# A new order of operations on every engine for a fused attention and MLP kernel

## The chip, the cores and the metric

The kernel runs on one core of a Trainium2 chip. The metric is the device time of one execution in microseconds; the time before is the median of three runs.

## The reference, cut to what matters

The input x is 2048 rows (S) of 448 columns (D) in bfloat16. Two blocks follow each other.

```python
h  = x + A(layernorm(x))          # local attention, 16 heads of 28, 8 keys at distances 0, 2, ..., 14
h2 = h + B(layernorm(h))

A: q, k, v = split(x @ wqkv)
   logits[s, w] = q[s] . k[s - 2w] / sqrt(28);  attn = softmax over w
   return (sum_w attn[s, w] * v[s - 2w]) @ wo

B: g = gelu(layernorm(x) @ w1);  shift the four quarters of g's columns by +1, -1, +2, -2 rows
   x1 = x + shifted(g) @ w2
   return x1 + gelu(layernorm(x1) @ w3) @ w4      # 448 -> 1792 -> 448
```

## The kernel before

The 2048 rows are worked in four tiles of 512 (t = 0 to 3), the last part of the MLP in five units of 256, 512, 512, 512 and 256 rows (u = 0 to 4). The phases of one tile carry names that the text uses:

- **N1, A1, V** (per t): layernorm of x; its transposition; q and k; v. The evicted v goes to `vt`, and up to four DMAs copy it with shifts into `vw`.
- **A2, S, A3, O**: A2 multiplies q by the shifted k on DVE (four products into `qk_r`; the three large ones 128 x 4096) and sums over the head on PE. S is the softmax; its last step is a product into `pb` that may run on DVE or on POOL. A3 spreads the weights on DVE (four products into `bd_r`) and multiplies them by `vw` on PE. O is the projection by wo and the residual.
- **B1, M**: two layernorms in one, normalisation into `lntm`, a transposition by DMA into `actT`, then the matmuls by w1 with gelu.
- **B2, T, W3, B3** (per u): shifted matmuls by w2 and the residual; layernorm and a transposition by DMA; the matmuls by w3 with gelu into `h3T`; the matmuls by w4, the last addition into `ost` and the DMA to the output.

All operations are first recorded, 891 of them, numbered 0 to 890 in the order of the phases. One number is an instruction or a group of matmuls. Then a list written out in the source, `ORDER` (line 19), gives the sequence: each engine works its own operations in that sequence, one after the other, and an operation that waits holds up all behind it on its engine. `OTHER` (line 51) names the operations that go to their second engine: an eviction from ACT to DVE, or a product from DVE to POOL. The list also decides which buffer an operation gets, since buffers are handed out and taken back along it: 8 PSUM banks, 3 `bd_r`, 2 `qk_r`, 2 `lntm`, 4 `actT`, 16 `h3T`.

All DMAs are issued by SP, in the order of the list. A transposition by DMA is kept apart from the loads and copies around it: `arrange` (lines 192 to 240) makes it wait until all of those ahead of it have landed, and makes those behind it wait until it has landed. Stores to the output are exempt.

```python
            if op.insts[0][0] == "dma_start_transpose":
                op.deps.update(turned + moved)
                turned, moved = [op], []
            elif op.is_dma and not callable(op.chan):
                op.deps.update(turned)
                moved.append(op)
```

All instructions are issued at line 994, so the profile's groups are told apart by the names of their tiles. The numbers that the text uses:

| number | what | engine before |
|---|---|---|
| 98, 101, 104, 106 | evictions of the first transposition (A1, t = 0) | ACT; 104 DVE |
| 127, 129 | evictions of the last q and k columns (t = 0) | DVE; ACT |
| 160, 161; 279, 280; 401, 402 | last step of the softmax's sum on ACT, and the product into `pb`, of S0, S1, S2 | 161 and 280 DVE, 402 POOL |
| 253 | copy of 128 x 48 in the arena (t = 1) | ACT |
| 256, 378, 379, 383 | evictions of v (t = 1, 2) | ACT |
| 368 | eviction of 64 x 256 (A1, t = 2) | ACT |
| 457 to 461 | variance of x for t = 3 (four squares, a logarithm) | ACT |
| 388, 390 | the first two large products of A2, t = 2 | DVE |
| 404, 521; 534, 411 | evictions of S2 and S3; of A3, t = 3 and 2 | ACT; 411 DVE |
| 505, 509 | large products of A2, t = 3; 506 and 510 are the matmuls on them | DVE |
| 420, 421, 424, 425 | residual of O, t = 2 | DVE |
| 200, 322, 440, 557 | transpositions of B1, t = 0 to 3, issued to M0, M1, M2, M3 | SP |
| 586, 649, 720, 791, 850 | transpositions of T, u = 0 to 4, issued to W3 | SP |
| 582, 583; 641 to 644 | normalisation of T0; of T1 | DVE |
| 501, 502, 503, 504 | copies of v of t = 3 into `vw` (16, 256, 320 and 48 KB) | SP |
| 35, 36; 37, 38 | loads of w3 (896 KB each); of w4 (784 KB each) | SP |
| 527, 528 | one of the A3 matmul groups of t = 3 and its eviction | PE; DVE |
| 617 | third of the four matmul groups of B3, u = 0 | PE |

Of the kernel before, what the change touches and what calls it, by code (L numbers as in the profile page):

```python
# [16 lines left out]
POWER = {'N1': 'aaaa', 'B1': 'aaaa', 'B2': 'apapp'}  # L17
RESIDUAL = 'ttvv'
ORDER = """
# [30 lines left out]
"""  # L50
OTHER = """
104 127 196 197 199 402 408 411 519 525 528 582 583
"""
FULL = (4,)
FILL = (1, 1, 0, 0)
# [980 lines left out]
```

## Time and profile before

| | |
|---|---|
| runs before | 194.11 us median (193.75 to 195.71, three runs) |
| span of the profiled execution | 192.0 us, 5741 instructions |
| PE, DVE, ACT, POOL busy | 181.2, 129.6, 133.0, 29.3 us |
| DMA moved | 17.04 MB, 89 GB/s in the mean |

The span runs from the first to the last instruction of the program; of the profiled execution the page gives the span alone, and the runs are longer than it by what lies before and after. A matmul's busy time overlaps with that of the next, so PE's share alone says little; whether one group follows the other without a hole is read from the rows in order of time. Groups of the view by line give a count, the busy time, the mean of one in ns and the idle time ahead of it.

### The profile page before, as it was taken

How to read it: one execution, taken by the hardware profiler on the slowest of the kernel's cores; microseconds unless marked ns; L12 is line 12 of the kernel's file. 1: busy time of each engine (PE TensorE's matmuls, PEld its weight loads, DVE VectorE, ACT ScalarE, POOL GpSimd, SP SyncE). 2: the span in 40 equal slices, each digit the busy share in tenths (PEclk: the TensorE clock that was granted, in tenths of full speed). 3: DMA queues.
4: the chain of work that ended last, by engine and by line, in shares of the span. 5: the costliest groups of instructions: out<-in, count | busy, mean ns of one | idle time of the engine just before them, and what ended most of it. 6: DMA issues, size and time to landing. Idle time of an engine off the chain costs nothing.

```text
span 192.0 us, 5741 instructions
## 1 busy us (share of the span) xinstructions
PE 181.2 (94%) x2482; PEld 92.6 (48%) x2482; DVE 129.6 (67%) x229; ACT 133.0 (69%) x310; POOL 29.3 (15%) x63
## 2 busy tenths in 40 slices
PE   6999999999999869969999999999999999999994
PEld 2584533453444333337545444455444544555672
DVE  7899999999999999999876970036988022002203
ACT  4489999999999999998595898860158004731340
POOL 3240000000004000201067000022077700000000
DMA  5998792005504163935905014006200542000111
GB/s 146 353 282 175 194 295 44 14 0 133 133 3 90 23 66 72 319 64 125 113 3 106 8 34 103 0 0 126 58 26 1 109 106 73 0 3 0 51 48 48
DMA packets 30273, 17.04 MB, mean 89 GB/s; under 512 B 18936, under 2 KB 29736, under 8 KB 30248
## 3 DMA queue, kind: packets, MB, share of 16 engines
q1 hardware_dynamic: 30248, 16.68, 37.1%
q8 instruction: 19, 0.31, 0.7%
q14 instruction: 6, 0.05, 0.1%
HBM read 8.04 MB, written 1.84 MB: 51 GB/s over the span
## 4 chain that ended last, share of the span: by engine, by line
PE 67%; DMA 13%; ACT 12%; DVE 3%; SPq 2%; issue 1%; POOL 0%; POOLq 0%; ACTq 0%
PE ps L994 67%; DMA actT<-lntm 7%; DMA arena<-in_B_w_dram 3%; ACT lntm L994 3%; ACT arena L994 3%; DMA vw<-vt 2%; ACT vt L994 2%; SPq L994 2%; DVE bd_r L994 2%; ACT h3T L994 1%; ACT actT L994 1%; ACT xin L994 1%; DVE lntm L994 1%; DVE ost L994 1%; ACT ls L994 1%
## 5 line engine op out<-in xcount | busy, mean ns | idle before, releaser
L994 PE MATMUL ps<-actT,arena 64*128 64x256 bf16 (+1 forms) x756 | 68.7, 329 | 2.2 <-DMA actT<-lntm 1.7
L994 ACT ACTIVATE h3T<-ps 128x512 bf16<-128x512 f32 (+1 forms) x70 | 30.3, 525 | 40.1 <-PE ps L994 40.0
L994 PEld LDWEIGHTS ps<-actT,arena 64*128 64x128 bf16 x756 | 35.4, 94 | 31.6 <-DMA actT<-lntm 2.1
L994 PE MATMUL ps<-arena,h3T 64*128 64x448 bf16 (+2 forms) x434 | 44.4, 343 | 0.0
L994 ACT ACTIVATE arena<-ps 128x512 bf16<-128x512 f32 (+10 forms) x86 | 40.1, 515 | 3.3 <-PE ps L994 2.5
L994 DVE SCALAR_TENSOR_TENSOR ost<-ps,mrs,arena 128x448 bf16<-128x448 f32 (+1 forms) x17 | 10.7, 652 | 36.5 <-PE ps L994 36.5
L994 DVE TENSOR_TENSOR qk_r<-arena 128x4096 bf16<-128x4096 bf16 (+1 forms) x16 | 32.0, 2016 | 0.4 <-ACT arena L994 0.2
L994 PEld LDWEIGHTS ps<-arena,h3T 64*128 64x128 bf16 (+1 forms) x434 | 23.0, 94 | 18.7 <-issue 0.2
L994 POOL TENSOR_TENSOR arena<-arena,xin 128x448 f32<-128x448 f32 x16 | 17.2, 1088 | 45.0 <-DVE lntm L994 45.0
L994 DVE TENSOR_TENSOR bd_r<-arena,bmask 80x2048 bf16<-80x2048 bf16 x16 | 19.0, 1216 | 1.6 <-PE ps L994 0.9
L994 ACT ACTIVATE actT<-ps 128x512 bf16<-128x512 f32 (+2 forms) x21 | 14.6, 742 | 2.1 <-PE ps L994 2.1
L994 PE MATMUL ps<-actT,w_s 64*128 64x512 bf16 x112 | 13.3, 377 | 1.7 <-DMA actT<-lntm 1.2
L994 PE MATMUL ps<-wo_s,actT 64*128 64x448 bf16 x128 | 14.3, 350 | 0.1
L994 PE MATMUL ps<-arena,actT 64*128 64x448 bf16 x112 | 12.4, 350 | 0.4 <-ACT vt L994 0.4
L994 PE MATMUL ps<-w_s,arena 64*128 64x448 bf16 x112 | 11.6, 350 | 1.0 <-ACT arena L994 0.9
L994 ACT ACTIVATE lntm<-xin,nm 128x448 bf16<-128x448 bf16 x16 | 10.5, 660 | 2.6 <-DVE nm L994 2.6
L994 DVE SCALAR_TENSOR_TENSOR arena<-xin,rs_y,ps 128x448 f32<-128x448 bf16 x16 | 10.3, 672 | 2.2 <-PE ps L994 2.2
L994 DVE TENSOR_SCALAR lntm<-arena,mv,rs_y 128x512 bf16<-128x512 f32 x14 | 10.2, 773 | 2.1 <-POOL rs_y L994 2.0
L994 POOL TENSOR_TENSOR pb<-ls,mx 128x512 bf16<-128x512 f32 x2 | 3.3, 1641 | 52.8 <-ACT mx L994 52.8
L994 DVE BATCH_NORM_STATS2 st<-xin 128x6 f32<-128x448 bf16 x16 | 9.4, 614 | 0.8 <-DMA xin<-in_A_x_dram 0.7
L994 PEld LDWEIGHTS ps<-actT,w_s 64*128 64x128 bf16 x112 | 5.1, 94 | 8.9 <-PE ps L994 1.7
L994 PEld LDWEIGHTS ps<-wo_s,actT 64*128 64x128 bf16 x128 | 5.6, 94 | 6.7 <-PE ps L994 1.4
(73 smaller groups left out, 161.7 us busy)
## 6 DMA issues: line engine op xcount, KB each, us to landing
arena<-in_B_w_dram SPq DMA_DIRECT2D x2, 896.0 KB, 7.3
out_dram<-ost SPq DMA_DIRECT2D x15, 112.0 KB, 1.9
arena<-in_B_w_dram SPq DMA_DIRECT2D x2, 784.0 KB, 5.7
vw<-vt SPq DMA_DIRECT2D x4, 320.0 KB, 4.3
vw<-vt SPq DMA_DIRECT2D x4, 256.0 KB, 4.2
arena<-in_A_wqkv_dram SPq DMA_DIRECT2D x2, 448.0 KB, 4.6
xin<-in_A_x_dram SPq DMA_DIRECT2D x2, 448.0 KB, 7.5
xin<-in_A_x_dram SPq DMA_DIRECT2D x3, 224.0 KB, 5.6
```

Source lines behind the costliest of these rows:

```text
L994: inst = getattr(eng, meth)(**kw)
```

## The change

Only `ORDER` and `OTHER` are replaced. No operation, buffer count or constant changes. Two lines of the old list and two of the new, and `OTHER` in full:

```diff
 ORDER = """
-43 8 7 2 11 0 1 49 44 45 6 9 10 12 5 39 13 40 42 58 59 60 61 63 64 62 70 68 50 51 52 53 54 55 56 57 14 65 66 71 69 67
-72 73 75 77 97 15 98 99 100 102 105 74 76 103 101 41 113 119 104 106 46 212 125 218 126 84 107 214 114 216 129 130 215
 ...
+0 1 49 50 51 52 53 54 55 56 57 39 40 2 7 5 42 8 58 59 60 61 11 9 63 64 62 65 66 10 68 70 71 67 69 6 41 72 73 74 75 97
+82 99 4 92 100 102 103 105 12 13 77 76 96 106 98 101 107 119 104 14 212 214 15 218 216 120 125 121 126 127 130 133 219
 ...
 OTHER = """
-104 127 196 197 199 402 408 411 519 525 528 582 583
+106 129 161 196 197 199 253 280 368 383 402 404 408 519 521 525 528 534 582 583
```

From `OTHER`: 106, 129, 253, 368, 383, 404, 521 and 534 go from ACT to DVE; 104, 127 and 411 go back to ACT; 161 and 280 go from DVE to POOL.

From `ORDER`, engine by engine, the places that the text speaks of:

```text
SP   before: ... 30..34 | 143 35 145 36 262 144 | 265 | 387 264 263 384 385 386 | 200 | 322 | 504 37 501 38 | 586 | 503 502 | 440 | 649 ...
SP   after:  ... 144 262 143 145 20 21 22 264 23 265 263 24..32 386 33 34 35 387 384 36 385 | 200 | 504 | 322 | 503 | 586 | 501 37 38 502 | 440 | 649 ...
DVE  before: ... 158 272 161 270 463..466 ... 277 388 392 280 390 185 ...
DVE  after:  ... 158 272 270 253 383 464 463 466 465 ... 277 388 368 390 392 185 ...
DVE  before: ... 505 308 310 304 306 (305 307 309 311) 412 406 415 321 320 319 318 409 509 574 575 576 411 507 408 581 425 424 511 583 582 420 421 ...
DVE  after:  ... 505 308 310 306 304 (311 309 307 305) 404 415 319 321 318 320 409 412 511 406 574 575 576 507 408 581 424 582 583 509 421 425 420 ...
PE   before: ... 615 616 | 530 533 524 | 447 441 448 442 (M2) | 527 | 617 | 535 539 536 540 | 618 | B22, W31 ...
PE   after:  ... 615 616 | 524 533 | 617 | 447 441 448 442 (M2) | 530 527 | 618 | 539 535 540 536 | B22, W31 ...
```

The bars on SP stand where a transposition and other DMAs wait for each other. In the tail (from W31 on) the matmul groups of W3, B3 and B2 change places among themselves, with their evictions.

56 rows, old and new, of the table ORDER are left out of this document.

## The prediction

> **What bounds the kernel now.** I read the page's shares first, then the busy time in five stretches, then the chain that ended last, then the single queues.
>
> ```profile
> span 192.0 us, 5741 instructions
> 13.80:63.60 49.80, 48.33 (x857) 22.51 (x854) 49.43 (x61) 49.42 (x130) 2.21 (x1) 1.00 0.46 109
> 63.60:85.70 22.10, 17.88 (x278) 7.04 (x278) 21.17 (x40) 21.69 (x47) 1.32 (x2) 1.00 0.52 114
> 85.70:96.10 10.40, 9.89 (x240) 7.08 (x242) 9.04 (x16) 7.54 (x23) 1.24 (x2) 1.00 0.68 110
> 96.10:192.00 95.90, 93.35 (x988) 48.46 (x988) 38.83 (x85) 46.56 (x93) 19.26 (x21) 1.00 0.20 45
> ```
>
> The columns are length, then PE, PEld, DVE, ACT and POOL busy. Up to 63.6 us DVE and ACT are full (49.4 of 49.8), and so nearly up to 85.7; PE has room there. From 96.1 on PE alone is full and nothing else is near it. So there are two kernels here: a front paced by the order on DVE and ACT, and a tail that is 96 us of matmuls without a hole, which a new order can't shorten, only start earlier or break. The chain tells what sets its start:
>
> ```profile
> 58.34 0.70 ACT lntm L994
> 64.01 3.49 DVE bd_r L994 x3
> 67.50 1.29 DVE lntm L994 x4
> 68.82 5.27 DMA actT<-lntm
> 74.78 0.57 SPq L994
> 76.09 6.49 DMA arena<-in_B_w_dram
> 82.60 3.06 DMA actT<-lntm
> 85.71 2.49 PE ps L994 x42
> 90.60 5.43 DMA actT<-lntm
> 96.07 92.72 PE ps L994 x981
> ```
>
> These are the transposition of B11 (68.82), the two loads of w4 (37 and 38, issued at 74.78 and 76.09), the transposition of T0 that had to wait for them (82.60), W30 (85.71), the transposition of B12 (90.60) and M2 (96.07), where the dense tail begins.
>
> **The change, part by part.** The work is the same 891 operations. I follow the new order up to M2 and ask how late or early each of those points comes.
>
> Engines. Two softmax products (161, 280) go from DVE to POOL, eight evictions or copies go from ACT to DVE, and three come back.
>
> ```profile
> L994 DVE TENSOR_TENSOR pb<-ls,mx 128x512 bf16<-128x512 f32 x2 | 1.4, 682 | 0.0
> L994 DVE CAST actT<-ps 128x512 bf16<-128x512 f32 x4 | 2.7, 683 | 0.0
> L994 DVE CAST arena<-ps 64x256 bf16<-64x256 f32 x1 | 0.4, 383 | 0.0
> 31.36 1.22 DVE L994 TENSOR_TENSOR qk_r<-arena 128x2048 bf16<-128x2048 bf16 x1
> 32.49 0.68 DVE L994 TENSOR_TENSOR pb<-ls,mx 128x512 bf16<-128x512 f32 x1
> 33.09 2.29 DVE L994 TENSOR_TENSOR qk_r<-arena 128x4096 bf16<-128x4096 bf16 x1
> ```
>
> Back to back, a DVE operation takes 0.08 less than its length (32.49 to 33.09 is 0.60 for one of 0.68). The pairs 104/106 and 127/129 only change places. Ahead of the normalisation of B10 DVE loses 161 and 280 (2 x 0.60) and gains 383 (0.55, from the 683 ns row scaled to 448), 368 (0.30) and 253, a copy of 128x48 that no row has on DVE (0.1 to 0.3, I take 0.2): -0.15 in sum. That is next to nothing on an engine that is full. ACT is relieved by the same three, which matters at B10 alone (below).
>
> The products on POOL are not free for DVE, though.
>
> ```profile
> 42.86 4.48 DVE L994 TENSOR_TENSOR qk_r<-arena 128x4096 bf16<-128x4096 bf16 x2
> 58.98 2.28 DVE L994 TENSOR_TENSOR qk_r<-arena 128x4096 bf16<-128x4096 bf16 x1
> 59.99 2.21 POOL L994 TENSOR_TENSOR pb<-ls,mx 128x512 bf16<-128x512 f32 x1 [47.99 <-ACT mx L994]
> 86.13 1.07 POOL L994 TENSOR_TENSOR pb<-ls,mx 128x512 bf16<-128x512 f32 x1 [4.84 <-ACT mx L994]
> 98.47 1.86 DVE L994 TENSOR_SCALAR lntm<-arena,mv,rs_y 128x512 bf16<-128x512 f32 x2 [1.14 <-POOL rs_y L994]
> 98.55 1.04 POOL L994 TENSOR_TENSOR arena<-arena,xin 128x448 f32<-128x448 f32 x1
> ```
>
> The product takes 1.07 when DVE reads PSUM beside it (86.13) and 2.21 when a DVE product of two SBUF tensors is under way (59.99: that one ends at 61.26, and 61.26 + 1.0 is where POOL ends). At 98.47 it is DVE that waits: two operations take 1.86 beside a POOL addition. So 280, whose input comes while 388 runs, waits for it and then holds up 390, since an eviction (368) stands between them and lets POOL in: 0.7 of its 1.07 on DVE. 161 comes some 2.5 later than the 32.49 of before (an estimate), because ACT now does 378, 256, 379, 460 and 461 ahead of 160; it meets 270's end and blocks the normalisations for 0.3. With the -0.15 and waits of 0.1 in the first 40 us, that is 0.95, and I say that DVE is 0.9 late by 505, which then ends at 62.1 instead of 61.26. If POOL takes nothing from DVE it is level; if each of 161, 280 and 402 takes its whole 1.07, it is 3.1 late. I take 0.9, the value nearest to the row at 59.99.
>
> [...]
>
> B10. Its transposition (200) waited at 58.34 + 0.70 = 59.04 for ACT's share of the normalisation, while DVE's was done at 58.3. Now ACT's is early and DVE's ends at 58.3 + 0.9 = 59.2. M0 comes at 63.6, as before. Ahead of 200 the SP queue now has the load of w3 behind V2's copies, which wait for A30 (43 by my walk); 2.5 MB at the pace of w4 below end at 56, 3 us to spare, and without them each microsecond costs one.
>
> B11 and T0. From 505's end to 322's issue it was 68.82 - 61.26 = 7.56. Two of the three bd products (3.49) now stand behind the normalisation and 404 (0.60) ahead of it: 5.83. So 322 is issued at 67.9 instead of 68.82 and lands at 73.2. T0's normalisation:
>
> ```profile
> 69.85 2.28 DVE L994 TENSOR_TENSOR qk_r<-arena 128x4096 bf16<-128x4096 bf16 x1
> 76.91 0.62 DVE L994 SCALAR_TENSOR_TENSOR xin<-ps,xin 128x448 bf16<-128x448 f32 x1
> 79.35 1.00 DVE L994 TENSOR_SCALAR lntm<-arena,nm,rs_y 128x512 bf16<-128x512 f32 x2
> 80.98 3.06 PE L994 MATMUL ps<-w_s,arena 64*128 64x448 bf16 x28 [0.23 <-ACT arena L994]
> 85.68 1.38 SPq L994 DMA_DIRECT2D vw<-vt  x2
> ```
>
> It ended at 80.35. Ahead of it are no longer 509 (2.20), 411 (0.60) and 425 (0.54), but 404 (0.60) and the 0.9: 78.5, less 0.4 for DVE's holes in that stretch, 78.1. 509 now comes behind it and ends at 80.3; the matmuls on it (510) come ahead of B21 on PE. So B21 starts at 81.0, as before (80.98), and W30 is free to start 2.65 later (B22, of the same size, goes from 105.35 to 108.00 below), at 83.65.
>
> The loads. 586 is issued at 78.1, with 503 landed before it (73.2 + 4.2), and lands 3.06 later, at 81.2. That is ahead of 83.65, so W30 starts at 83.65 instead of 85.71: **2.05 won**. But w4, 501 and 502 are now behind 586, and B12's transposition (440) waits for all of them. Before, w4 went from 74.78 to 82.58: 7.8. Now: 81.2, one short copy, w4 from 81.9 to 89.7, and 502 behind it.
>
> ```profile
> vw<-vt SPq DMA_DIRECT2D x4, 256.0 KB, 4.2
> DMA to landing us min/median/max: 2.2/4.2/8.3
> DMA to landing us min/median/max: 3.0/4.4/5.4
> ```
>
> The second row is that of vw, the third that of actT. 502 has 256 KB. At w4's pace (1568 KB in 7.8) it adds 1.3, and 440 is issued at 91.0; it takes 8.3 at the most from its issue at 83.2, 91.5; it adds its whole 4.2 if it runs only when w4 is done, 93.9. I take 91.0. B12's normalisation itself is ready a little earlier, at 90.3 by the same count of DVE's operations. 440 took 5.43 in this place, so M2 starts at 96.4 instead of 96.07. Of the 2.05 nothing is left there.
>
> What stays is work done ahead of M2.
>
> ```profile
> 96.07 3.20 PE L994 MATMUL ps<-actT,w_s 64*128 64x512 bf16 x28 [0.43 <-DMA actT<-lntm]
> 99.20 0.42 PE L994 MATMUL ps<-bd_r,vw 80*32 80x64 bf16 x32
> 99.55 1.50 PE L994 MATMUL ps<-arena,h3T 64*128 64x448 bf16 x14
> 105.35 2.81 PE L994 MATMUL ps<-w_s,arena 64*128 64x448 bf16 x28
> 108.00 10.74 PE L994 MATMUL ps<-actT,arena 64*128 64x512 bf16 x98
> ```
>
> 617 (1.44, from 99.55 to 100.99) now goes ahead of M2, one more A33 group (0.3) behind it. From M2 to B22 it was 9.28; it becomes 8.14, so B22 starts at 104.5 instead of 105.35. W31, 2.65 later, needs T1's transposition: DVE's 528 stands ahead of three of T1's four normalisations and waits for 527 on PE (about 100), so 649 is issued at 102.2 to 103.1 and lands 4.4 later, at 106.6 to 107.5. W31 starts at 107.25 instead of 108.00. This wait is a cover that is nearly gone: each later microsecond of 649 costs one.
>
> The tail. From W31 on the same matmuls follow. Walking banks, transpositions and gelus, I find the next tight place at W32, about 1 us of slack for T2 (its last normalisation now stands behind an operation on B23). I cost it at nothing; without the slack it costs what T2 is late.
>
> The sum: 192.0 - 0.75 = 191.25 in the span. The median of the runs is 194.11, 2.1 more than the span; that lies around it and stays: 191.25 + 2.1 = **193.4 us**. An error of 1 us in 440's issue moves it by 1.
>
> **The rivals.**
>
> 1. *Faster, 191.9.* POOL takes nothing from DVE (T0 at 77.2) and 440 takes the median 4.4 instead of 5.43. Then not the landing but PE starts M2, at about 95.0, 1.4 earlier than in the sum. For it: B11's and B12's are the only long ones of nine. Against: B12's stood behind copies then as it will now.
>
> 2. *Slower, 196.3.* The copy 502 makes no headway until w4 is through: 89.7 + 4.2 = 93.9, M2 at 99.3, B22 at 107.4, W31 at 110.1 or a little later, 2.2 behind: 192.0 + 2.2 + 2.1. For it: copies of vw have taken up to 8.3, and w4 alone takes 7.8. Against: two of them together took only 4.9 (issued at 85.68, and 440, which waited for both, at 90.60). It costs time from M2 later than 97.1 on, and over 1% from 99.0.
>
> 3. *Little, but slower, 195.5.* POOL gets its turn after every DVE product, and 161, 280 and 402 cost DVE 3.1 instead of 0.9. T0, and with it w4 and M2, come 2.2 later: 193.4 + 2.2 - 0.1. The rows at 42.86 and 33.09 show how close the DVE products stand, for it; against it, 160 is so late that 161 meets fewer of them.
>
> 4. *The change doesn't do what it says, 194.1.* DVE is full and its work is the same; the w4 move wins at W30 what it loses at M2, and 649 takes the rest.
>
> **How the numbers follow.** The forecast with its own range of 192.6 to 194.3 gets 0.36, rival 4 0.10, the first 0.18, the second 0.24, the third 0.12. A change under about 1% (1.9 us) can't be told from none here: faster is the first rival and a little of the forecast (0.20), slower the second and a quarter of the third (0.27), the rest is within it (0.53). Range 191.3 to 196.6: from below rival 1 to above rival 2.
>
> **What would show it.** Right: W30 at about 83.6, with T0's transposition issued before w4; DVE rows beside POOL's pb lengthened; 440 at 91, waiting for a DMA; PE full from M2 on, with at most a short wait at W31. Wrong: B10's transposition waiting for w3, B21 later than 82, a hole at W32, or B12's normalisation later than 91.

## The result and the profile after

The changed kernel takes 203.76 us (median of four runs, 203.37 to 204.92) beside 194.06 for the kernel before in the same series: ratio 1.0488, 95% interval 1.0430 to 1.0545. It is slower by 9.7 us, where 193.4 (191.3 to 196.6) was predicted. Its profiled execution has a span of 201.5 against 192.0. First the page of the changed kernel: the busy time, and the granted clock in 40 slices.

```profile
PE 185.8 (92%) x2482; PEld 95.2 (47%) x2482; DVE 130.7 (65%) x232; ACT 134.4 (67%) x305; POOL 38.5 (19%) x65
PEclk9999999999979997899999999999999999999999
```

DVE and ACT have about as much work as before (130.7 and 134.4 against 129.6 and 133.0); PE has 4.6 us more busy time for the same 2482 matmuls, and the clock row is lowered in three slices, at two places. The busy time in stretches of the changed kernel, cut at the same events as before (start of the dense front, M0, W30, M2, end); the last three columns are the granted clock, the DMA share and GB/s:

```profile
13.80:71.10 57.30, 51.35 (x855) 22.98 (x856) 49.91 (x59) 51.56 (x130) 8.88 (x4) 0.97 0.39 101
71.10:93.40 22.30, 18.68 (x280) 7.64 (x282) 20.46 (x39) 20.44 (x40) 1.27 (x1) 0.92 0.32 68
93.40:105.40 12.00, 11.32 (x224) 7.39 (x222) 11.85 (x25) 11.04 (x28) 3.90 (x3) 1.00 0.65 178
105.40:201.50 96.10, 92.70 (x1008) 49.84 (x1004) 37.72 (x83) 44.06 (x90) 19.17 (x21) 1.00 0.23 45
```

The lengths were 49.8, 22.1, 10.4 and 95.9: the loss is 7.5 ahead of M0, 0.2 up to W30, 1.6 up to M2, and 0.2 in the tail. In the first stretch DVE does as much as before (49.9 against 49.4) in 7.5 us more, so it stands idle there; the clock is 0.97 and 0.92 where it was 1.00. The chain that ended last in the changed kernel shows which waits are new:

```profile
47.00 6.29 POOL pb L994
...
79.67 7.31 PE ps L994 x84
87.01 2.87 DVE qk_r L994
...
111.34 5.61 DMA actT<-lntm
```

A POOL product, PE itself in the middle of the front, and a product of DVE stand where the chain of before, from 43.07 to 85.71, had ACT, short stretches of DVE, copies, the loads of w4 and the transpositions. The pieces around 47 in the changed kernel, by engine in order of time. A row gives start, length, engine and operation, and in brackets how long the engine had stood idle and what ended it:

```profile
35.82 1.48 POOL L994 TENSOR_TENSOR pb<-ls,mx 128x512 bf16<-128x512 f32 x1 [23.69 <-ACT mx L994]
36.29 1.05 DVE L994 COPY arena<-arena 128x48 bf16<-128x48 bf16 x1
...
45.34 2.27 DVE L994 TENSOR_TENSOR qk_r<-arena 128x4096 bf16<-128x4096 bf16 x1
47.00 6.28 POOL L994 TENSOR_TENSOR pb<-ls,mx 128x512 bf16<-128x512 f32 x1 [9.70 <-ACT mx L994]
47.54 0.41 DVE L994 CAST arena<-ps 64x256 bf16<-64x256 f32 x1
47.87 4.47 DVE L994 TENSOR_TENSOR qk_r<-arena 128x4096 bf16<-128x4096 bf16 x2
53.43 0.49 PE L994 MATMUL ps<-ident,pb 64*80 64x64 bf16 x16 [2.92 <-POOL pb L994]
54.88 1.76 PE L994 MATMUL ps<-arena,actT 64*128 64x448 bf16 x8
56.38 0.17 DVE L994 TENSOR_SCALAR nm<-mv 128x4 f32<-128x4 f32 x1 [4.04 <-ACT xin L994]
```

Operation 280 has its input at 47.00 and ends at 53.28. It got its turn neither at the end of 388 (47.61) nor beside the eviction 368 (47.54) nor between 390 and 392; it ends 0.94 after the end of the last of them (52.34). Transposition 281 on PE needs it and stood first on that queue for 2.92; the matmuls of O0 stand behind 281, their results go through ACT, and DVE's next operation, 185, waited 4.04 for those. 161 (35.82) takes 1.48 on POOL, and the copy 253 beside it 1.05.

### The profile page after: what moved, and what is told of

It reads as the page before. It is cut to its first block, busy times and chain, and to the rows that moved or that the text cites. A ratio compares the mean times of both kernels' runs of the same rounds, so it can differ in the third digit from the quotient of the medians.

```text
span 201.5 us, 5745 instructions
## 1 busy us (share of the span) xinstructions
PE 185.8 (92%) x2482; PEld 95.2 (47%) x2482; DVE 130.7 (65%) x232; ACT 134.4 (67%) x305; POOL 38.5 (19%) x65
## 4 chain that ended last, share of the span: by engine, by line
PE 53%; ACT 19%; DVE 18%; DMA 4%; POOL 3%; issue 2%
PE ps L994 53%; ACT arena L994 10%; DVE qk_r L994 4%; ACT actT L994 3%; POOL pb L994 3%; DMA actT<-lntm 3%; DVE lntm L994 3%; DVE bd_r L994 2%; DVE st L994 2%; DVE arena L994 2%; ACT lntm L994 2%; DVE mx L994 1%; ACT vt L994 1%; ACT xin L994 1%; DMA xin<-in_A_x_dram 1%
## 5 line engine op out<-in xcount | busy, mean ns | idle before, releaser
L994 PE MATMUL ps<-actT,arena 64*128 64x512 bf16 (+1 forms) x756 | 69.6, 329 | 1.6 <-DMA actT<-lntm 0.8
L994 PEld LDWEIGHTS ps<-actT,arena 64*128 64x128 bf16 x756 | 36.2, 94 | 30.7 <-PE ps L994 2.0
L994 ACT ACTIVATE arena<-ps 128x512 bf16<-128x512 f32 (+9 forms) x83 | 39.6, 507 | 10.7 <-PE ps L994 9.7
L994 PE MATMUL ps<-arena,h3T 64*128 64x448 bf16 (+2 forms) x434 | 45.5, 343 | 0.0
L994 POOL TENSOR_TENSOR arena<-arena,xin 128x448 f32<-128x448 f32 x16 | 18.3, 1154 | 58.0 <-DVE lntm L994 58.0
L994 POOL TENSOR_TENSOR pb<-ls,mx 128x512 bf16<-128x512 f32 x4 | 9.9, 2477 | 56.4 <-ACT mx L994 56.4
L994 DVE TENSOR_SCALAR lntm<-arena,mv,rs_y 128x512 bf16<-128x512 f32 x14 | 8.0, 610 | 12.7 <-ACT rs_y L994 12.1
L994 PE MATMUL ps<-arena,actT 64*128 64x448 bf16 x112 | 13.8, 369 | 0.4 <-ACT arena L994 0.2
L994 PE MATMUL ps<-w_s,arena 64*128 64x448 bf16 x112 | 13.3, 373 | 0.4 <-ACT arena L994 0.3
L994 DVE SCALAR_TENSOR_TENSOR arena<-xin,rs_y,ps 128x448 f32<-128x448 bf16 x16 | 10.4, 676 | 3.8 <-PE ps L994 3.7
L994 PE MATMUL ps<-qk_r,zc 128*32 128x512 bf16 x112 | 8.7, 400 | 1.1 <-DVE qk_r L994 1.1
```

The lines of the kernel that those rows point to most:

```text
L994: inst = getattr(eng, meth)(**kw)
```

## Experiments

`OTHER` and `ORDER` are edited; times are medians beside the kernel before of the same series. A ratio and its interval are not the quotient of the two medians. "Filler" stands for matmuls of 128 x 512 that nothing reads.

### The products back on DVE

```diff
-106 129 161 196 197 199 253 280 368 ...     # changed kernel
+106 129 196 197 199 253 368 ...             # both; the second kernel takes out 280 alone
```

> The changed kernel with the two softmax products 161 and 280 on DVE again, all else as changed. Theory A (the product 280 on POOL got no turn while DVE's products followed each other, 6.28 us instead of 1.07, and PE stood at 281 behind it with O0's matmuls and DVE's 185): DVE's wait of 4.04 us ahead of 185 falls to about 1, since PE is busy with 181 until 50.5 in any case; that is 3.0 off the end. The copy 253 is back from 1.05 to 0.23, the two products cost DVE 1.2. If the matmuls after PE's pause (497 took 1.76 instead of 0.92) are also back, another 1.7. Sum 203.8 - 3.0 (- 1.7) + 0.3: 199.2 to 201.0, so the product is half of the loss or less. Theory B (the loss comes from the order of evictions and DMAs; the product only fills a wait that is there anyway): 203 to 204.

> The changed kernel with only 280 on DVE again; 161 stays on POOL. Theory A (280 is the dear one, 161 costs only what the copy 253 waits, 0.8 against 0.6 won): as with both on DVE within 0.5, 199.2 to 201.3. If 161 is as dear as 280, this one stays 1.5 or more above the one with both on DVE. Theory B: 203 to 204.

With both on DVE: 199.36 (196.84 to 199.53), 1.0204 [1.0104, 1.0305]. With 280 alone on DVE: 199.28, 1.0246 [1.0171, 1.0320]. So 280 on POOL costs 4.4 us (203.8 less 199.4), and 161 on POOL nothing that can be told. In the first kernel's timeline the product takes 0.68 between the same neighbours, and 185 stands at 53.12, not 56.38:

```profile
47.93 0.68 DVE L994 TENSOR_TENSOR pb<-ls,mx 128x512 bf16<-128x512 f32 x1
...
53.12 0.17 DVE L994 TENSOR_SCALAR nm<-mv 128x4 f32<-128x4 f32 x1
```

The other 5.3 us lie elsewhere. Then the reverse, the kernel before with 280 on POOL:

```diff
-104 127 196 197 199 402 ...
+104 127 196 197 199 280 402 ...
```

> The kernel before, with only 280 put on POOL. Its input is there at 44.6, in the first of three products (388, 392, 390) that now follow each other on DVE from 42.86 to 49.5. Theory A (POOL gets no turn in an unbroken chain): the product is recorded from 44.6 to about 50.4, 5.8 long, 281 starts at 50.4 instead of 48.68, and the kernel is 1.0 to 1.7 slower, 195.1 to 195.8. The prediction's theory (POOL takes its turn behind the product under way): recorded at 1.5 to 2.2, done by 46.2, one DVE product lengthened by up to 1, DVE 0.6 relieved: 193.7 to 194.5.

194.47 (193.57 to 196.50), 1.0010 [0.9971, 1.0048]: no difference that can be told. In its timeline the product is long here too:

```profile
42.59 4.48 DVE L994 TENSOR_TENSOR qk_r<-arena 128x4096 bf16<-128x4096 bf16 x2
44.40 3.61 POOL L994 TENSOR_TENSOR pb<-ls,mx 128x512 bf16<-128x512 f32 x1 [32.93 <-ACT mx L994]
47.69 2.46 DVE L994 TENSOR_TENSOR qk_r<-arena 128x4096 bf16<-128x4096 bf16 x1 [0.62 <-PE ps L994]
```

It comes during the first of two products, misses the turn at that one's end and ends 0.94 after the second (47.07). But its result is there at 48.01, and 281 stood at 48.68 before: the order of before had cover for it, the new one has none. The theory that POOL gets no turn came true in part: it had one only where DVE stood waiting (0.62), and that was early enough.

### When POOL gets its turn

Small kernels with DVE chains and the POOL product alone, to measure the disputed cost by itself. T is the 128 x 4096 product, D the 80 x 2048 one, e an eviction; the number is how much earlier or later POOL's input comes.

```diff
-(the whole of the work)
+PATTERNS: 0:TTTT 0:TeTTT 0:TcTTT 0:DDDDD 0:TTTTTTTT ...   # one POOL product beside each
```

> No attention and no MLP is computed (the output is x): only the POOL product 128x512, started during the first of a chain of DVE operations, in 29 patterns. T is the large product of A2, D that of A3, e an eviction 64x256 and E one of 128x512 from PSUM, b statistics, c the copy 128x48, n a normalisation, r a reduction from PSUM. Theory A (a chain without a break starves POOL): in TTTT the product ends 0.9 after the last T, 7 to 9 us long, and T stays at 2.28; in TcTTT it ends 0.9 after the first T and c is lengthened to about 1, as 253 was; in TeTTT it is starved as behind 368. The prediction's theory (POOL takes its turn at the first end): 0.9 after the first T in all of them, and the T or X that follows is lengthened by up to 1. [...] If what counts is the length of the opening, E, ee and eee let it in where e does not.

In 28 of the 29 patterns POOL got its turn at the end of the product under way, with or without something between the T: it ends 0.93 to 0.94 after that one, and what follows on DVE is longer for it (a T behind an eviction takes 2.83 instead of 2.28, the copy c 1.04). In the 29th no product was under way, and POOL took 1.07. The starvation was not there. Was it that the chain lacked semaphore waits?

```diff
+PATTERNS: 0:TTTT 0:T?TTT 0:T!TTT ...   # no wait, a wait already met (?), a real wait (!)
```

> Chains of DVE operations beside one POOL product again (no attention and no MLP is computed, the output is x), but now the operations write to different buffers, so that they don't wait for each other, as 388, 368, 390 and 392 didn't. Marks: ? is a wait that was met long before, ! a wait for the operation just ahead; T is the large product, D that of A3, e an eviction of 128 columns, c the copy 128x48, n a normalisation. Theory W (POOL gets the turn only where the next DVE operation is not queued yet when the one under way ends): in TTTT, T?TTT, TeTT, TeeTT and DDDD the product is recorded until 0.9 after the last operation (7 to 9 us for TTTT, 3 to 4 for DDDD) and no T is lengthened; in T!TTT it ends 0.9 after the first T, and the second T is lengthened by 0.8, as in the first chains. The first theory (a turn at each end): 0.9 after the first T in all of them. If any wait, met or not, opens the turn, T?TTT goes as T!TTT. For c and n the case of 253 says that they let POOL in and are lengthened by 0.8.

Again POOL came at the first end in each of 26 patterns, here the first:

```profile
39.83 2.28 DVE L984 TENSOR_TENSOR qk_r<-arena 128x4096 bf16<-128x4096 bf16 x1
40.57 2.47 POOL L984 TENSOR_TENSOR pb<-ls,mx 128x512 bf16<-128x512 f32 x1 [38.99 <-ACT mx L984]
```

39.83 + 2.28 = 42.11, and the product ends at 43.04. Waits are not it. Third, earlier and later inputs, T that feed matmuls, evictions on ACT, matmuls and DMAs beside them:

```diff
+PATTERNS: 0::TTTT ... 9::TTTT  4:A:TTTT 4:M:TTTT 4:G:TTTT 4::FFFF 4:AGM:FFFF ...
```

> Chains of large products beside one POOL product a third time (no attention and no MLP is computed, the output is x), because in both earlier chain runs POOL always got its turn at the end of the product under way, while 280 in the changed kernel and in the kernel before with 280 on POOL got none behind 388. Changed here: the start of the POOL product within the first T in steps of about 0.2 (0 to 9); F, a T with its PE matmuls behind it and a semaphore; A, 12 evictions on ACT beside it; G, matmuls on PE beside it; M, loads and copies by DMA beside it; the operands of tile 2. Theory L (a product that starts less than about 0.6 before the end of the one under way misses the turn): the leads 3 to 5 show 3 to 5 us in place of 1.2 to 1.6, the others not, whatever goes on beside. Theory M (DMA traffic holds POOL off): the patterns with M alone. Theory A or G: those alone. [...] If none does, the cause is not among these.

None of them starved POOL: it came at the first end, or just behind the next T when its input came so late (durations of 1.07 to 3.07). What all these chains had in common was a DVE that had waited right ahead of them. The fourth put ten D and the reductions of a real softmax without a wait ahead of T:

```diff
+PATTERNS: :TTT :aTTT :aaTTT F:TTT ... FA:TTT FA:TeTT   # ten D and the softmax's reductions ahead; a: POOL's input later by one ACT operation
```

> The POOL product beside chains a last time (no attention and no MLP, the output is x), now as 280 stood in the kernel: ahead of the chain DVE works ten products of A3, a reduction and a subtraction from PSUM without a wait, POOL has been idle for over 10 us, the chain is TTT or TeTT into the two buffers of qk_r, with (F) and without matmuls of PE on each product, evictions on ACT (A), DMA traffic (M). [...] If POOL again gets its turn behind the first T everywhere, what starves 280 in the kernel stays open.

Here it is. The timeline of that kernel, two of its patterns:

```profile
70.32 6.68 DVE L1010 TENSOR_TENSOR qk_r<-arena 128x4096 bf16<-128x4096 bf16 x3
71.06 15.96 POOL L1010 TENSOR_TENSOR pb<-ls,mx 128x512 bf16<-128x512 f32 x1 [69.48 <-ACT mx L1010]
76.92 9.16 DVE L1010 TENSOR_TENSOR bd_r<-arena,bmask 80x2048 bf16<-80x2048 bf16 x8
87.05 0.69 DVE L1010 TENSOR_REDUCE mx<-ps 128x64 f32<-128x512 f32 x1 [0.97 <-POOL pb L1010]
...
92.99 6.88 POOL L1010 TENSOR_TENSOR pb<-ls,mx 128x512 bf16<-128x512 f32 x1 [5.97 <-ACT mx L1010]
```

In the first POOL waits through three T and eight D until DVE itself has to wait for it (0.97): 15.96 for work of 1.07. In the second it starts during the first of three T and ends 0.93 after the third. Patterns in which DVE has a wait in the chain gave 4.68, and those in which an eviction had to wait 2.48. So POOL can be kept off for as long as DVE runs without a break (15.96); that a product waits 6.28 needs nothing particular to the changed kernel. Which of the things put ahead of T does it is not shown, since they came together; a wait of 0.73 that ended 3.5 us ahead of T, which three patterns with matmuls on the D had, did not help (6.88 and 6.89). What decides between 6.88 and 15.97 is open too: with POOL's input later by none, one and two ACT operations the same chain of three T gave 15.96, 6.88 and 15.97.

That POOL, once waiting, has the turn at the end of the DVE instruction under way agrees with the products that start during a T and end 0.93 after it; the rows of 6.28 and 15.96 don't agree. The row at 98.47, in which the prediction has DVE wait, is a TENSOR_SCALAR with one large input (1.86 for two beside the POOL addition, 1.00 at 79.35 without one) and no product of two.

### Where the other 5.3 us are

Three kernels take the order and engines of before up to a point and the changed ones behind it.

```diff
-ORDER = changed
+ORDER = before's up to 268 (28.6 us) | 505 (59.0) | 583 (80.4), then the changed list without those
+OTHER = by the part in which the operation stands; 161, 280 on DVE
```

> The order and engines of before up to 268 (the first 28.6 us), the changed ones behind it, with 161 and 280 on DVE. Compared with the changed kernel with both products on DVE (199.4), this gives back DVE's waits ahead of 223, 151 and 456 (1.8 more than before in the first 30 us). Theory A (those waits go through to the end): 388 at 43.8 instead of 45.4, and 197.5 to 198.2. Theory B (they are taken up by the later waits of DVE): 199 to 199.6.

197.83 (196.63 to 198.38), 1.0179 [1.0121, 1.0236]. Against the kernel with both products on DVE (199.36) the first 28.6 us cost 1.5; the two were measured in different series. The changed kernel's DVE rows that belong to it:

```profile
12.38 1.32 DVE L994 TENSOR_SCALAR lntm<-xin,mv,rs_y 128x448 bf16<-128x448 bf16 x4 [0.93 <-ACT rs_y L994]
22.41 2.29 DVE L994 TENSOR_TENSOR qk_r<-arena 128x4096 bf16<-128x4096 bf16 x1 [0.72 <-PE ps L994]
29.48 0.17 DVE L994 TENSOR_SCALAR nm<-mv 128x4 f32<-128x4 f32 x1 [0.58 <-ACT lntm L994]
```

> The order and engines of before up to T0's normalisation (583), the changed ones behind it (T0's transposition ahead of w4, 502 behind w4, 617 ahead of M2, the tail). The prediction's steps, with no front loss: T0's transposition issued at 80.4, W30 at 83.5 to 83.9 instead of 85.71, M2 at 96.1 to 96.5, W31 at 107.3 to 108.2, and 193.0 to 194.8. Its second rival (502 only after w4): M2 at 98 or later, 195.5 to 196.5. If the tail is what costs (its own 0.5 to 1 between W31 and the end): W31 as said and 194.5 to 195.5.

195.54 (194.70 to 197.01), 1.0074 [1.0030, 1.0117]: this is what remains when only the order of w4 and the tail is changed, 1.6 us. Its chain:

```profile
80.48 3.59 DMA actT<-lntm
85.95 6.94 DMA vw<-vt
92.91 4.32 DMA actT<-lntm
97.27 3.89 PE ps L1002 x92
103.27 6.00 DMA actT<-lntm
```

T0's transposition goes ahead of w4, as said, and W30 starts at 84.12 instead of 85.71. Then 502, issued behind w4, takes 6.94; 440, which waits for it, is issued at 92.91 instead of 90.60, M2 stands at 97.27 (+1.2), and T1's transposition takes 6.00, so that W31 starts at 109.41 (+1.4).

> The order and engines of before up to 505 (58.98), the changed ones behind it. Theory A (the order behind 505 is the second half of the loss: 509 no longer fills DVE's wait for B20, whose matmuls end at 71.9 in any case, so taking it away brings T0's normalisation forward by next to nothing, and behind that normalisation 509 now holds up the matmuls 510 and B21): DVE waits 1 to 1.6 ahead of 574, T0's normalisation ends at 80.2 to 80.8, B21 starts at 84 to 85 instead of 80.98, W30 at 86.7 to 87.7, and the kernel is 3.5 to 4.5 slower, 197.5 to 198.5. Theory B (the loss is all from ahead of 505): B21 at 81, W30 at 83.7, 193.4 to 194.6.

198.94 (197.96 to 199.39), 1.0238 [1.0174, 1.0301]: 5.0 us more than the 193.89 of the kernel before in this series, of which 3.4 (198.94 less 195.54) come between 505 and T0 in an order that has neither the first 30 us nor the POOL products of the change. This was the surprise. Its timeline, DVE and PE:

```profile
63.71 0.63 DVE L1002 BATCH_NORM_STATS2 st<-xin 128x6 f32<-128x448 bf16 x1 [1.89 <-ACT xin L1002]
68.13 0.42 PE L1002 MATMUL ps<-bd_r,vw 80*32 80x64 bf16 x32 [1.61 <-DVE bd_r L1002]
70.56 0.62 PE L1002 MATMUL ps<-bd_r,vw 80*32 80x64 bf16 x32 [1.26 <-DVE bd_r L1002]
72.36 3.04 PE L1002 MATMUL ps<-w_s,arena 64*128 64x448 bf16 x14
75.44 0.68 DVE L1002 SCALAR_TENSOR_TENSOR arena<-xin,rs_y,ps 128x448 f32<-128x448 bf16 x1 [1.53 <-PE ps L1002]
```

DVE waits 1.89 for ACT, PE waits 1.61 and 1.26 for DVE, and then two groups of B20 take 3.04 together (1.74 before) and DVE waits 1.53 for them. The busy time of the same kernel in stretches, with the granted clock in the third column from the end:

```profile
67.00:71.00 4.00, 1.61 (x70) 0.95 (x70) 4.00 (x7) 3.94 (x6) 0.00 (x0) 0.92 0.08 16
71.00:75.00 4.00, 3.37 (x62) 1.33 (x52) 2.91 (x3) 3.91 (x7) 0.00 (x0) 0.50 0.63 121
```

PE is busy 1.61 of 4 us, and right behind it the clock is 0.50. In finer stretches it is 0.50 from 70.3 to 77.1, 6.8 us; in the changed kernel it is so twice for 3.4, from 54.4, behind the pause for 280, and from 78.3.

### Is it the clock?

That the clock is lowered by PE's pauses was until here an argument. The test leaves every operation of the last kernel in its place and fills the pauses:

```diff
+S.tag = "gate"
+for n in (5, 4, 2):                      # behind 201, 202 and 410 on PE
+    b = _Tile(P_bank)
+    mms([(b(), ident[:], bass.AP(ident, 0, [[128, 128], [0, 4], [1, 128]]), True, True, 512, None)] * n)
```

> The kernel with the old order up to 505 and the changed one behind it (198.9), with 11 matmuls more that nobody reads, put where PE idles between M0 and B20 (behind 201, 202 and 410). Theory A (PE's idling there, 3.4 of 6 us, lowers the granted clock to 0.5 at B20, and that is part of the loss): PEclk stays near 1 from 71 to 79, B20's two groups take 1.7 to 2.0 instead of 3.0, T0's normalisation comes 1 earlier, and the kernel takes 197.5 to 198.3. Theory B (the clock follows something else, or the fillers hold up the matmuls behind them): 198.9 or more.

195.10 (194.61 to 195.72), 1.0043 [1.0011, 1.0075]: more work on PE, 3.8 us less than the 198.94 without it, a larger gain than was expected. In stretches:

```profile
67.00:71.00 4.00, 3.28 (x79) 1.28 (x77) 4.00 (x7) 3.92 (x7) 0.00 (x0) 1.00 0.12 24
71.00:75.00 4.00, 3.51 (x61) 1.45 (x61) 3.78 (x6) 3.93 (x6) 0.00 (x0) 1.00 0.59 113
```

The clock is 1.00 in both. In all ten runs the mean granted clock was 0.999 or 1.00, in the four without fillers 0.982 to 0.991. The time is also no more than the 195.54 of the old front to T0, so with the clock held the order between 505 and T0 costs nothing that can be told. Kernels without fillers show the same from run to run: with both products on DVE three runs at 0.991 took 199.28 to 199.53, and the one at 1.00 took 196.84. The kernel before loses a little too: in the last series 13 of its 22 runs were at 0.991, with a median of 194.22, and nine at 0.999 or 1.00, with 193.61. Its profiled execution was one without a loss.

The same on the changed kernel itself, with 21 fillers: 12 behind 181 (the pause for 280), 5 behind 202, 3 behind 410, 1 behind 413.

> The changed kernel, order and engines untouched, with 21 matmuls more that nobody reads where PE idles: 12 in the pause behind 181 (50.5 to 53.4, while 280 is awaited), 9 behind 202, 410 and 413. Theory A (the granted clock falls because PE idles, and the matmuls after the two idle stretches are then at up to half speed): PEclk 1.00 throughout, the matmuls behind the pause 1.7 shorter, those of B20 and O2 back to 0.93 and 0.74, and 203.8 falls to 198.0 to 199.5, by which the clock is half of the loss. Theory B (only the waits themselves count): 203 or more.

199.57 (199.16 to 200.39), 1.0274 [1.0212, 1.0336], 4.2 us less than without. The POOL product is as long as ever, but the group behind it is fast (1.76 in the changed kernel, 0.95 here):

```profile
55.41 0.95 PE L1007 MATMUL ps<-arena,actT 64*128 64x448 bf16 x8
```

Then together with the other causes:

```diff
 both products on DVE, fillers behind 202, 410, 413 (5, 3, 1)
 the same, and the first 28.6 us of before
```

> The changed kernel with 161 and 280 on DVE (199.4) and 9 matmuls that nobody reads behind 202, 410 and 413. Theory A: the clock stays up, and 195.2 to 196.4 remains, which is the waits of the first 30 us (0.9 to 1.5) and the order of w4 and 502 (1.6, as the old front with the changed order from T0 on has shown). Theory B: 198.5 or more, the clock's loss shown in the mixed order is not in this one.

> The changed kernel with three parts undone at once: the first 28.6 us in the old order, 161 and 280 on DVE, and 9 matmuls that nobody reads behind 202, 410 and 413. If the parts add up as measured (197.2 with the last two, and 1.5 for the first 30 us), 195.4 to 196.0 is left, and that is what the old front with the changed order from T0 on takes (195.5). If the waits of the first 30 us are taken up later, 197 as before.

197.17 (196.39 to 197.65), 1.0141 [1.0087, 1.0194], and 196.43 (195.01 to 197.67), 1.0105 [1.0074, 1.0137]. Both a little above what was expected. So the parts of the 9.7 are: fillers alone take away 4.2, the product put back alone 4.4, both 6.6, since the pause behind 280 lowers the clock too and 2.0 is in both. Of the 3.1 that are left (197.17 less 194.06), the first 28.6 us have 0.7 with the clock held (1.5 without), and w4's order about 1.6; some 0.8 is placed by no run. The kernel before had medians of 193.89 to 194.63 in these series, so parts smaller than that difference are uncertain.

### A version that beats both

What was right in the change is T0's transposition ahead of the second half of w4. Done alone in the order of before:

```diff
-SP: 200 | 322 | 504 37 501 38 | 586 | 503 502 | 440
+SP: 200 | 504 503 | 322 | 501 502 37 | 586 | 38 | 440      and 617 ahead of M2
```

> The kernel before with SP's order changed alone and 617 ahead of M2: 504 and 503 behind B10's transposition; 501, 502 and the first half of w4 behind B11's; the second half of w4 behind T0's. By the walk through the rows of before: T0's transposition issued at 80.4 instead of 82.6, W30 at 83.6 to 84.1 instead of 85.7, 440 at 89.4 to 90.1, M2 with 617 ahead of it at 95.2 to 95.9, W31 at 106.6 to 107.0 instead of 108.0, and 192.6 to 193.3. Rival: B11's transposition waits for the copies 503 and 504, or T1's transposition, which hangs on DVE, sets W31 at 108 as before: 193.8 to 194.5.

193.81 (193.02 to 195.26), 0.9974 [0.9945, 1.0004], short of the 192.6 to 193.3 expected. Its profiled execution was the slowest of its twelve runs (195.26) and had a granted clock of 0.78 from 69 to 75, where the kernel before had 1.00 in its profiled execution with the same pauses on PE (0.42, 0.60 and 0.68):

```profile
69.00:75.00 6.00, 4.57 (x106) 2.02 (x110) 5.64 (x10) 5.87 (x13) 0.00 (x0) 0.78 0.63 91
```

So five fillers in those pauses (2 behind 416, 3 behind 413), once with the split and once without:

> The kernel before with w4's loads split around T0's transposition and 617 ahead of M2 (193.8 so far), and 5 matmuls more that nobody reads behind 416 and 413, since the granted clock fell to 0.78 at 69 to 75 us in that run. Theory A (the clock's dip took what the earlier transposition won): PEclk 1.00, T0's transposition issued at 80.4, W31 at 106.6 to 107.2, and 192.4 to 193.2. Theory B (T1's transposition or DVE sets the tail's start whatever PE does): 193.6 to 194.2.

> The kernel before with 5 matmuls that nobody reads behind 416 and 413 and nothing else. Its profile showed PEclk 1.00, so theory A (the clock falls in some executions only, since PE's pauses of 0.42, 0.60 and 0.68 us are just short of it) expects the median unchanged to 0.4 less, 193.6 to 194.2, and fewer runs above 195. Theory B (the split of w4 had no share in 193.45, the fillers had all): 193.3 to 193.6.

With the split 193.45 (193.21 to 196.39), 0.9939 [0.9908, 0.9971]: 0.6% faster than the kernel before and the best of all, but not the 192.4 to 193.2 expected. The fillers in the kernel before gave 193.93, 1.0008 [0.9974, 1.0042]: by themselves nothing that can be told, and four of the twelve runs were still above 195. How much of the 0.6% is the order is not settled: 15 of the 17 runs of the kernel before in that series had a clock of 0.982 to 0.991, eleven of the twelve with the split and fillers 0.999 or 1.00. Between the profiled executions, both at 1.00, W31 starts at 107.44 instead of 108.00, and the span is 191.5 instead of 192.0. The queue of SP in the split kernel with fillers:

```profile
80.85 1.27 SPq L1007 DMA_TRANSPOSE actT<-lntm  x1
89.71 13.39 SPq L1007 DMA_TRANSPOSE actT<-lntm  x2
```

T0's transposition goes at 80.85 (82.60 before), the second half of w4 behind it at 83.97, and B12's at 89.71 (90.60 before): both are earlier, since only one half of w4 is ahead of each.

## Why the prediction was wrong, step by step

**The products on POOL** (term 0.9): wrong in its mechanism. The step took the row at 59.99, one turn behind one product, and said that the eviction 368 lets POOL in, which no row of before shows, and that DVE then pays 0.7. The runs showed POOL waiting through 388, 368, 390 and 392, and the price at the reader of the product: 2.92 on PE, 4.04 on DVE, 4.4 in the time. The third rival had POOL win each turn and DVE pay for it, the opposite sign. The copy 253, priced at 0.2, took 1.05 beside 161 (1.48); 161 on POOL cost nothing in the time that can be told.

**Waits of 0.1 in the first 40 us**: mis-sized. 268 stood 1.59 later (30.16 for 28.57; waits of 0.93, 0.72 and 0.58 that the order of before did not have in this size), 388 at 45.34 instead of 42.86. In the time 0.7 to 1.5.

**B10** (200 at 59.2): 65.68. Of its condition, that w3's loads don't hold it, nothing failed: it waited for the normalisation. The 6.5 are those of the two steps above.

**B11** (5.83 from 505's end to 322's issue): 6.52 in the changed kernel, 8.17 with the front of before, where the statistics of B11 wait 1.89 and 0.61 for copies that ACT now does behind four evictions. The step counted what DVE no longer had ahead of it, and did not ask whether ACT's part was there.

**T0 at 78.1** (509's 2.20 taken out): the step that turned the forecast's gain into nothing. It counted DVE's own work and did not ask when what DVE waits for is ready. DVE's next operation, 574, needs B20 from PE, and in the timeline of before it follows at once:

```profile
69.05 0.42 PE L994 MATMUL ps<-bd_r,vw 80*32 80x64 bf16 x32 [0.60 <-ACT arena L994]
70.15 1.74 PE L994 MATMUL ps<-w_s,arena 64*128 64x448 bf16 x14 [0.68 <-ACT arena L994]
72.05 0.67 DVE L994 SCALAR_TENSOR_TENSOR arena<-xin,rs_y,ps 128x448 f32<-128x448 bf16 x1
```

B20 ended at 71.89 and 574 stood at 72.05, so unless B20 came earlier too, taking out 509 could bring 574 forward by 0.2 at most. In the kernel with the old front to 505 DVE then waits 1.53 for B20, but most of that is the slow clock. With fillers there the wait is 0.22, B20 takes 1.74, and T0's normalisation ends at 79.8, where the forecast's steps give 77.2 on a front that is not late:

```profile
73.98 0.68 DVE L1007 SCALAR_TENSOR_TENSOR arena<-xin,rs_y,ps 128x448 f32<-128x448 bf16 x1 [0.22 <-PE ps L1007]
78.80 1.00 DVE L1007 TENSOR_SCALAR lntm<-arena,nm,rs_y 128x512 bf16<-128x512 f32 x2
```

By the count the waits of 1.89 and 0.61 for ACT at B11 make 2.5 of the 2.6 between them. And 509 itself, now behind the normalisation, holds B21: 83.65 there, with the clock at 1.00, for 80.98. The changed kernel's timeline:

```profile
76.16 0.42 PE L994 MATMUL ps<-bd_r,vw 80*32 80x64 bf16 x32 [1.19 <-DVE bd_r L994]
77.38 0.42 PE L994 MATMUL ps<-bd_r,vw 80*32 80x64 bf16 x32 [0.81 <-DVE bd_r L994]
78.12 2.86 PE L994 MATMUL ps<-w_s,arena 64*128 64x448 bf16 x14 [0.32 <-ACT arena L994]
```

509 (87.01) takes 2.87 with a POOL addition beside it, B21 starts at 90.69, and the prediction had "later than 82" among the signs that it is wrong.

**The granted clock** was no term at all: it stood at 1.00 in every stretch of the profiled execution of before, and no step asked what would become of it when PE pauses. The rows above show what it does: PE waits 1.19, 0.81 and 0.32, and B20 takes 2.86 instead of 1.74. This was the term of 4.2 us, about as dear as the product, with 2.0 in both. In the kernel with the old front to 505 no single gap from 58 us to B20 was over 1.61, and behind two (1.61 and 1.26) the clock fell to 0.50; in the changed kernel it did so behind 2.92, and behind 1.19, 0.81 and 0.32: several short gaps brought the same 0.50 as one of 2.92. Nor do pauses of one size always give the same clock: those of the split kernel, of the size of before (0.42, 0.60 and 0.68), gave 0.78, and those of before 1.00. Why is not shown.

**The loads, 502 and B12** (440 issued at 91.0, 12.9 behind T0's transposition at 78.1): this step held. With the old front to T0 it stands by itself: T0's transposition, issued at 80.48, landed in 3.59 instead of 3.06, and 440 went at 92.91, 12.4 later. w4 and 502, issued from 84.71 on, had landed after 8.2, where the chosen bound gives 9.1 (81.9 to 91.0) and the second rival 12.0 (81.9 to 93.9). The 6.94 of 502 runs beside the loads. What costs the 1.6 there is the premise: w4 and 440 now stand behind T0's normalisation, which in that kernel is no earlier than before (80.35), and M2 comes at 97.27 instead of 96.07. The prediction's gain hung on the 2.25 that T0 did not win. In the changed kernel 440 was issued at 100.40 because DVE was late with B12's normalisation, and M2 (105.35) did not wait for it.

**617 ahead of M2**: right. From M2 to B22 it was 8.14 (105.35 to 113.49), as worked out. **The cover at W31**: thin, as said, and gone: 649 took 5.6 to 6.0 instead of 4.4, and PE waits 0.8 there, which takes back most of what 617 won. **The tail**: nearly right, dense behind W31, and 84.4 from there to the end instead of 84.0.

## What to carry to other kernels

Before an operation is taken out from ahead of a deadline, look whether the next ones on the engine will be ready: where a releaser ended just before, or was itself put later by the change, what is removed becomes a wait. A product on POOL beside DVE's products has no fixed price (1.07 of work took 1.48 to 15.96 here); ask when its result is read, and give it slack for the whole unbroken run of DVE. A front that is paced by other engines can still cost matmul time: short pauses of PE close together can lower the granted clock for what follows (0.50 behind 1.61 and 1.26), and a few matmuls that nothing reads, put into the pauses, may be cheaper than the pauses (3.8 us less with eleven).

## What the runs showed of the hardware

- POOL's product of 1.07 took 1.48, 2.21, 3.61, 6.28 and 15.96 beside DVE products of two SBUF tensors. In the small patterns whose chain began right behind a wait of DVE, POOL came at the end of the product under way, every time; behind ten products and a softmax's reductions it came two or three products on, or not until DVE stopped. What decides between these is open.
- Behind pauses of PE of 1.61 and 1.26, with 1.2 us of work between them, the granted clock was 0.50 for 6.8 us. With eleven unread matmuls in these pauses and the next it stayed at 1.00, and the kernel took 3.8 us less. How much pause it takes is not shown.
- A transposition into `actT` took 3.06 (T0, 256 rows) to 6.00 (T1, 512 rows), and a copy of 256 KB issued behind the 1568 KB of w4 6.94 where two copies together had taken 4.9.
